# Accumulating transfers in place of VectorE additions in a Strassen matmul chain

## The chip, the cores and the metric

One core of a Trainium2 chip runs the kernel. The metric is the time of one execution on the device, in microseconds (us). Each run of a kernel gives one time; a median of runs is compared with a median. One execution is also recorded by the hardware profiler; its span goes from the first to the last instruction.

## The reference, cut to what matters

```python
# attention: 4 batches, 12 heads, 448 positions, 64 per head
scores = cap * tanh(q @ k.T / sqrt(64) / cap); attn = softmax(scores); x = attn @ v
# mixer 1: over tokens, then over channels (768 -> 1536 -> 768)
u  = x + (relu(x.T @ w_tok1) @ w_tok2).T
x  = u + relu(u @ w_ch1) @ w_ch2
# mixer 2: real part of a two-dimensional FFT, normalization, channels (768 -> 3072 -> 768)
u  = x + real(fft(fft(x, axis=1), axis=2))
un = (u - mean(u)) / sqrt(var(u) + 1e-6)
out = u + relu(un @ w_ch1) @ w_ch2
```

All of it is fp32.

## The kernel before

An fp32 product is made of three matmuls at reduced precision: each factor is split into a high part and a low part (`wh`, `wl` for weights; `u`, `r`, `y` tiles for activations), and `mm3` (L300 to L303) adds high x high, high x low and low x high in PSUM. The split takes one copy on ScalarE (L329) and one subtraction (L332) on VectorE or, where the planner prefers it, on GpSimd.

The stages follow each other: attention with the token mixer (to about 300 us), the first channel mixer, the FFT as matmuls with tables, and the second channel mixer. The result accumulates in SBUF in `z`: 12 tiles `z[bp][kc]` of 128 channels x 2 x 448 positions, `bp` being a pair of batches, `kc` one of six groups of channels. When a PSUM tile `mm` is complete, `gather` (L1555) adds it to `z`, on VectorE: the instruction z<-mm,z.

The second channel mixer does its first pair of batches as ordinary products and, for the second pair, uses Strassen's scheme: seven products in place of eight, per group of hidden channels `g`. `up_steps(g)` makes the seven hidden operands out of sums and differences, `down_steps(o, g)` the seven products with the second weight. While this second half runs, the tiles `z[0][...]`, whose own result has been stored, serve as accumulators `a` for products that belong into more than one place:

- products 1 and 5 collect in `a = z[0][kc]`, kc = 0 to 2 (`a[:, 0, :]` and `a[:, 1, :]`); 
- products 6 and 7 collect in `a = z[0][NJ + kc]`, with NJ = 3.

The accumulators are then folded into `z[1]`. At the end of the group before the last, `fold_in` (L1597) adds the two halves of `a` to each other and the whole of `a` to `z[1][kc]` and to `z[1][NJ + kc]`; `fold_out` (L1604) does likewise for products 6 and 7. In the last group the accumulators start from zero again, and `last15` (L1612) and `last67` (L1622) copy the first PSUM half into `a` (ScalarE), add the second (VectorE), and fold. `last23` (L1633) gathers products 2 and 3 and stores; product 4 goes by `one` (L1586). Each store waits for all additions to its tile.

No engine's program is written out by hand. All operations are first listed with what they read and write, and a planner (`Plan.run`, L187) then picks the next one again and again: it has a cost for each operation on each engine, a lag until the result of a transfer can be used, and starts whatever can begin first. Ties and near ties go by a rank, the place in the list shifted by the tables `SHIFT` (by stage) and `FINE` (by 64 operations of a kind). It counts a cost for TensorE's change between kinds of matmul (`LEAVE`, `ENTER`, L224) and keeps GpSimd apart from VectorE's instructions on SBUF. Each engine then works through its list in order, waiting for semaphores. GpSimd's list holds the maxima over partitions of attention, a part of the subtractions, and eight loads of FFT tables (L841, L857), the only transfers that it issues; all others are issued by SyncE (SP).

Of the kernel before, what the change touches and what calls it, by code (L numbers as in the profile page):

```python
# [56 lines left out]
class Op:  # L57
# [8 lines left out]
    None: -2, "acc0": -4454, "acc1": 433, "all": 12, "all<": -585, "all>": 551, "av": 161, "av<": -4361,  # L66
# [3 lines left out]
    "den>": -1057, "dev0": -4528, "dev1": -728, "exp": 272, "exp<": -611, "exp>": -1228, "fold00": 27,  # L70
    "fold01": -173, "fold02": -771, "fold10": -37, "fold11": 219, "fold12": -777, "gather": -43, "hid": -327,
    "late": 605, "load": -427, "load<": 151, "load>": -1918, "max": 70, "max<": -6696, "max>": -3403,
    "mean0": -1187, "mean1": -6750, "mix1": 211, "mix2": 266, "mix1>0": -3128, "mix1>1": -150, "mix2>1": 113,
    "mixh": -1004, "mixh>0": -68, "mixh>1": 41, "norm": -902, "norm<": 288, "norm>": -2108, "piece": -88,
    "recip": -63, "recip<": -608, "recip>": -179, "row0": -5, "row1": -1713, "scores": -39, "scores<": -1930,
    "scores>": -120, "spec00": -4598, "spec01": -978, "spec10": 399, "spec11": 251, "su0": 326, "su1": -368,
    "sub": -237, "sub<": -271, "sub>": -7902, "tanh": 187, "tanh<": -2194, "tanh>": 145, "tmm00": 130,
    "tmm01": -1093, "tmm10": 311, "tmm11": -1096, "tok1": 276, "tok2": -2798, "tokens00": -28, "tokens01": -5846,
    "tokens02": 2, "tokens10": 224, "tokens11": -318, "tokens12": -4780, "turn": -5524, "turn<": -1352,
    "turn>": -3039, "wx": -65, "xt": -5606, "xt<": -991, "xt>": -3434,  # L80
}
FINE = {
# [42 lines left out]
class Plan:  # L125
# [10 lines left out]
    LEAVE = {"rows": 0.11, "cols": 0.08}  # L136
    ENTER = 0.09
# [125 lines left out]
def kernel(  # L263
# [67 lines left out]
    def tt(engs, out, in0, in1, op, reads, writes):  # L331
        pl.op(engs, lambda e: eng[e].tensor_tensor(out=out(), in0=in0(), in1=in1(), op=op), reads, writes)  # L332
# [411 lines left out]
    def phase_ce():  # L744
# [851 lines left out]

        def fold_in(kc):  # L1597
            a, zl, zh = z[0][kc], z[1][kc], z[1][NJ + kc]
            ka = zk(0, kc)
            tt(v(S), lambda: a[:, 1, :], lambda: a[:, 1, :], lambda: a[:, 0, :], ALU.add, ka[:1], ka[1:])  # L1600
            for x, k in ((zl, kc), (zh, NJ + kc)):
                tt(v(W2), lambda x=x: x, lambda x=x: x, lambda: a, ALU.add, ka, zk(1, k))

        def fold_out(kc):  # L1604
            a, zl, zh = z[0][NJ + kc], z[1][kc], z[1][NJ + kc]
            ka = zk(0, NJ + kc)
            tt(v(S), lambda: zl[:, 1, :], lambda: zl[:, 1, :], lambda: a[:, 0, :], ALU.add, ka[:1], zk(1, kc)[1:])
            tt(v(S), lambda: a[:, 1, :], lambda: a[:, 1, :], lambda: a[:, 0, :], ALU.add, ka[:1], ka[1:])
            tt(v(W2), lambda: zh, lambda: zh, lambda: a[:, 1:2, :].to_broadcast([128, 2, S]), ALU.add, ka[1:],
               zk(1, NJ + kc))  # L1610

        def last15(kc, ps):  # L1612
# [6 lines left out]
            for x, k in ((zl, kc), (zh, NJ + kc)):  # L1619
                tt(v(W2), lambda x=x: x, lambda x=x: x, lambda: a, ALU.add, ka, zk(1, k))  # L1620
# [257 lines left out]
```

## Time and profile before

| | us |
|---|---|
| median of 3 runs | 1386.49 (1384.38 to 1386.78) |
| the profiled execution | 1383.64 |
| its span | 1381.9 |
| TensorE (PE) busy | 1359.3 |
| VectorE (DVE) busy | 973.6 |
| ScalarE (ACT) busy | 713.3 |
| GpSimd (POOL) busy | 300.7 |

PE is the engine of matmuls, PEld its weight loads, which run beside it. A matmul's own duration overlaps with the next one's, so the pace is read from start to start. In a row of the timeline stand start, duration, engine, line, operation, out<-in and, in brackets, idle time of the engine before it and what ended it. Where several like instructions stand in one row, x2 tells their number and the duration is that of all. The granted clock of TensorE is 1.00 at its upper level, 2.4 GHz, and 0.50 at the lower, 1.2 GHz.

### The profile page before, as it was taken

The page shows a single profiled execution, that of the slowest core. Times are in us where ns is not written, and L with a number is a line of the kernel's source. Part 1 is how long each engine was busy: PE and PEld are TensorE (multiplying, and loading weights), DVE is VectorE, ACT ScalarE, POOL GpSimd, SP SyncE. Part 2 cuts the span into 40 slices and gives each one's busy share as a digit, 9 for nine tenths or more (in the row PEclk, how much of TensorE's full clock was granted, in tenths as well). Part 3 has the DMA queues.
Part 4 walks back from the last instruction along what each step waited for, and adds up shares of the span by engine and source line. Part 5 has one row for each costly group of instructions (what it writes and reads, how often), then busy time and mean ns, then how long its engine had stood idle before and what let it go on. Part 6 is the DMA issues. An engine that isn't in the chain of part 4 may idle for free.

```text
span 1381.9 us, 18670 instructions
## 1 busy us (share of the span) xinstructions
PE 1359.3 (98%) x7470; PEld 1133.6 (82%) x7470; DVE 973.6 (70%) x1006; ACT 713.3 (52%) x836; POOL 300.7 (22%) x159
## 2 busy tenths in 40 slices
PE   8899999999999999999999999999999999999997
PEld 3345454589999999899989989999999999999987
DVE  7898787745564555658888687677676646756697
ACT  7888887766566444123223335544554553543432
POOL 3342342300000001000002242425123313212311
PEclk9999999999999999999999999999999999999999
DMA  4221321025666465512241177988778433344452
GB/s 125 89 74 54 105 63 54 21 92 161 227 236 220 161 229 187 166 67 92 69 160 58 42 256 269 334 276 309 249 257 299 133 117 102 105 129 144 126 181 94
DMA packets 67352, 211.89 MB, mean 153 GB/s; under 512 B 7552, under 2 KB 8960, under 8 KB 67266
## 3 DMA queue, kind: packets, MB, share of 16 engines
q1 hardware_dynamic: 66112, 208.08, 45.1%
q0 software_dynamic: 1152, 2.62, 0.7%
q8 instruction: 59, 0.97, 0.3%
q14 instruction: 27, 0.22, 0.0%
q10 hardware_dynamic: 2, 0.00, 0.0%
HBM read 145.30 MB, written 65.37 MB: 152 GB/s over the span
## 4 chain that ended last, share of the span: by engine, by line
PE 95%; ACT 2%; DVE 1%; DMA 1%; issue 0%; DVEq 0%; ACTq 0%
PE mm L301 25%; PE mm L303 25%; PE mm L302 25%; PE av L588 6%; PE sc L520 5%; PE av L604 3%; PE mx L715 2%; DMA wl<-kept 1%; ACT t L525 1%; PE av L615 1%; PE mx L711 1%; PE mx L301 1%; PE mx L303 1%; PE mx L302 1%; ACT t L545 1%; DVE z L332 1%
## 5 line engine op out<-in xcount | busy, mean ns | idle before, releaser
L303 PE MATMUL mm<-u,wl 128*128 128x448 f32 x786 | 287.2, 365 | 1.6 <-DMA wl<-kept 1.6
L301 PE MATMUL mm<-u,wh 128*128 128x448 f32 x786 | 287.6, 366 | 0.9 <-issue 0.7
L302 PE MATMUL mm<-u,wh 128*128 128x448 f32 x780 | 285.5, 366 | 0.0
L332 DVE TENSOR_TENSOR z<-mm,z 128x896 f32<-128x896 f32 (+1 forms) x211 | 214.8, 1028 | 79.3 <-PE mm L303 76.6
L301 PE MATMUL mm<-r,wh 128*128 128x448 f32 x696 | 254.7, 366 | 0.3 <-ACT wh L329 0.3
L303 PE MATMUL mm<-r,wl 128*128 128x448 f32 x696 | 254.5, 366 | 0.3 <-DVE wl L332 0.3
L302 PE MATMUL mm<-r,wh 128*128 128x448 f32 x654 | 239.1, 366 | 0.0
L303 PEld LDWEIGHTS mm<-u,wl 128*128 128x128 f32 x786 | 147.6, 188 | 14.3 <-DMA wl<-kept 2.0
L301 PEld LDWEIGHTS mm<-u,wh 128*128 128x128 f32 x786 | 147.6, 188 | 14.0 <-issue 1.4
L302 PEld LDWEIGHTS mm<-u,wh 128*128 128x128 f32 x780 | 146.5, 188 | 11.8
L301 PEld LDWEIGHTS mm<-r,wh 128*128 128x128 f32 x696 | 130.8, 188 | 11.9 <-ACT wh L329 0.6
L303 PEld LDWEIGHTS mm<-r,wl 128*128 128x128 f32 x696 | 130.7, 188 | 11.4 <-DVE wl L332 0.7
L537 POOL PARTITION_ALL_REDUCE mb<-m x48 | 95.9, 2049 | 169.6 <-DVE m L332 149.1
L302 PEld LDWEIGHTS mm<-r,wh 128*128 128x128 f32 x654 | 122.9, 188 | 10.4 <-DVE r L332 0.4
L329 ACT ACTIVATE r<-mm 128x896 fp32r<-128x896 f32 (+5 forms) x85 | 70.0, 828 | 109.0 <-PE mm L303 56.7
L329 ACT ACTIVATE cva<-raw 128x768 bf16<-128x768 int8 (+2 forms) x76 | 67.4, 887 | 96.1 <-DMA raw<-in_m_dram 49.2
L332 DVE TENSOR_TENSOR t<-t,mb 112x1792 f32<-112x1792 f32 x48 | 105.5, 2228 | 8.6 <-POOL mb L537 8.6
L332 POOL TENSOR_TENSOR wl<-wl,wh 128x768 fp32r<-128x768 f32 x18 | 36.1, 2008 | 344.1 <-ACT wh L329 344.1
L525 ACT ACTIVATE t<-sc,scl 112x896 f32<-112x896 f32 x96 | 93.1, 1010 | 17.0 <-PE av L604 8.1
L329 ACT ACTIVATE wh<-wl 128x768 fp32r<-128x768 f32 x57 | 48.2, 845 | 93.9 <-DMA wl<-kept 92.1
L520 PE MATMUL sc<-qr 64*112 64x448 f32 x384 | 89.5, 576 | 6.2 <-ACT t L525 5.2
L545 ACT ACTIVATE t<-t,cap_sb 112x1792 f32<-112x1792 f32 x48 | 85.6, 1791 | 10.8 <-DVE t L332 10.6
(203 smaller groups left out, 2158.3 us busy)
## 6 DMA issues: line engine op xcount, KB each, us to landing
raw<-in_m_dram SPq DMA_DIRECT2D x48, 767.6 KB, 5.2
wl<-kept SPq DMA_DIRECT2D x85, 384.0 KB, 3.6
kept<-u SPq DMA_DIRECT2D x60, 384.0 KB, 5.0
raw<-in_c_dram SPq DMA_DIRECT2D x24, 767.6 KB, 5.4
kept<-y SPq DMA_DIRECT2D x32, 384.0 KB, 5.3
raw<-kept SPq DMA_DIRECT2D x31, 384.0 KB, 3.1
wh<-kept SPq DMA_DIRECT2D x28, 384.0 KB, 3.3
qr<-in_qk_dram SPq DMA_DIRECT2D x23, 448.0 KB, 3.3
```

What stands on the lines that cost most here:

```text
L301: T.matmul(out=dst, lhsT=wh, rhs=xh, start=first, stop=False, skip_group_check=more)
L302: T.matmul(out=dst, lhsT=wh, rhs=xl, start=False, stop=False, skip_group_check=more)
L303: T.matmul(out=dst, lhsT=wl, rhs=xh, start=False, stop=last, skip_group_check=more)
L329: pl.op(a(n), lambda e: A.activation(out=out(), in_=src(), func=func, **kw), reads, writes)
L332: pl.op(engs, lambda e: eng[e].tensor_tensor(out=out(), in0=in0(), in1=in1(), op=op), reads, writes)
L520: T.matmul(out=ps()[:CP, k, :S], lhsT=qr()[d, S + c * CP:S + (c + 1) * CP], rhs=qr()[d, :S], start=True, stop=True)
L525: pl.op(a(W2, 0.06), lambda e, c=c, ps=ps: A.activation(out=tl()[:, c], in_=ps()[:CP, :, :S], func=AF.Tanh, scale=scl[:CP, 0:1]), [ps, tl] ...
L537: pl.op({"P": 1.9}, lambda e, k=k: P.partition_all_reduce(mb()[:, k], mx()[:, k], CP, bass_isa.ReduceOp.max), [mx, mb], [kb], hold=0.75)
L545: pl.op(a(2 * W2, 0.1), lambda e, k=k: A.activation(out=tl()[:, :, k], in_=tl()[:, :, k], func=AF.Exp, scale=cap_sb[:CP, 0:1]), [tl], [ke])
L588: T.matmul(out=ps()[d, :S], lhsT=vv()[:, c, d], rhs=tl()[:, c, hd], start=(c == 0), stop=(c == NCH - 1))
L604: T.matmul(out=ps()[32 * k:32 * k + 32, :S], lhsT=ones[:CP, 0:32].bitcast(F32), rhs=tl()[:, c, hd], start=(c == 0), stop=(c == NCH - 1))
L715: T.matmul(out=ps()[:, :S], lhsT=channels_of(rt()[:, tb, c], kc % NJ), rhs=wt[:, tb, :], start=False, stop=last, skip_group_check=True)
```

## The change

The additions of a whole accumulator, or of one half of it, to a tile of `z[1]` leave VectorE. In their place GpSimd issues a transfer from SBUF to SBUF which adds to its destination. The planner gets a cost of 0.6 us for GpSimd and a lag of 5.0 us. The addition inside `a` stays on VectorE. `SHIFT` and `FINE` (101 and 304 numbers) are replaced throughout, and the costs of a change between kinds of matmul are altered, so all engines' lists are in a new order.

```diff
 SHIFT = {
-    None: -2, "acc0": -4454, "acc1": 433, "all": 12, "all<": -585, "all>": 551, "av": 161, "av<": -4361,
+    None: -2, "acc0": -4783, "acc1": 438, "all": 11, "all<": -387, "all>": 21, "av": 151, "av<": -4659, "av>": 181,
...
 FINE = {
-    "A_0": -211, "A_1": -967, "A_2": -275, "A_3": 2, "A_4": 26, "A_5": -68, "A_6": -37, "A_7": -23, "A_8": 43,
+    "A_0": -75, "A_1": -959, "A_2": -237, "A_3": 17, "A_4": -35, "A_5": -87, "A_6": 35, "A_8": 82, "A_9": -43,
...
-    LEAVE = {"rows": 0.11, "cols": 0.08}
-    ENTER = 0.09
+    LEAVE = {}
+    ENTER = 0.095
...
+        def plus(o, i, reads, writes):
+            pl.op({"P": 0.6}, lambda e: P.dma_start(out=o(), in_=i(), accum_op=ALU.add), reads, writes, lag=5.0)
+
         def fold_in(kc):
...
             for x, k in ((zl, kc), (zh, NJ + kc)):
-                tt(v(W2), lambda x=x: x, lambda x=x: x, lambda: a, ALU.add, ka, zk(1, k))
+                plus(lambda x=x: x, lambda: a, ka, zk(1, k))
 
         def fold_out(kc):
...
-            tt(v(S), lambda: zl[:, 1, :], lambda: zl[:, 1, :], lambda: a[:, 0, :], ALU.add, ka[:1], zk(1, kc)[1:])
+            plus(lambda: zl[:, 1, :], lambda: a[:, 0, :], ka[:1], zk(1, kc)[1:])
             tt(v(S), lambda: a[:, 1, :], lambda: a[:, 1, :], lambda: a[:, 0, :], ALU.add, ka[:1], ka[1:])
-            tt(v(W2), lambda: zh, lambda: zh, lambda: a[:, 1:2, :].to_broadcast([128, 2, S]), ALU.add, ka[1:],
-               zk(1, NJ + kc))
+            plus(lambda: zh, lambda: a[:, 1:2, :].to_broadcast([128, 2, S]), ka[1:], zk(1, NJ + kc))
```

`last15` changes as `fold_in` does, `last67` as `fold_out`. `S` is 448, `W2` 896 columns. Each of the four functions is called for three kc.

## Rows read from the trace of the kernel before

**Rows 1.** The page: busy us of each engine, share of the span, instructions.
```profile
PE 1359.3 (98%) x7470; PEld 1133.6 (82%) x7470; DVE 973.6 (70%) x1006; ACT 713.3 (52%) x836; POOL 300.7 (22%) x159
```

**Rows 2.** Busy time by stretch: stretch, length, busy us (instructions) per engine, clock, DMA.
```profile
0.00:50.00 50.00, 43.26 (x248) 17.40 (x250) 40.77 (x35) 39.11 (x40) 20.93 (x15) 0.97 0.35 106
300.00:1300.00 1000.00, 995.96 (x5044) 917.98 (x5043) 663.28 (x703) 447.11 (x539) 181.94 (x96) 1.00 0.53 179
1300.00:1344.00 44.00, 44.00 (x218) 40.67 (x217) 38.99 (x41) 15.66 (x18) 13.18 (x6) 1.00 0.50 160
1344.00:1352.00 8.00, 5.31 (x19) 4.42 (x18) 8.00 (x9) 3.89 (x6) 0.00 (x0) 0.79 0.30 109
...
1374.50:1382.00 7.50, 0.04 (x1) 0.00 (x0) 3.75 (x6) 0.00 (x0) 0.00 (x0) 0.78 0.61 234
```

**Rows 3.** Waits of TensorE over the span: us in total, times, longest.
```profile
PE mm L302 <- DVE r L332: 2.7, 1, 2.7
PE mm L303 <- DMA wl<-kept: 1.6, 1, 1.6
```

**Rows 4.** Timeline of TensorE, about 1344 to 1352 us.
```profile
1344.26 0.37 PE L301 MATMUL mm<-y,raw 128*128 128x448 f32 x1
1347.32 0.47 PE L302 MATMUL mm<-r,raw 128*128 128x448 f32 x1 [2.69 <-DVE r L332]
...
1351.05 0.53 PE L301 MATMUL mm<-r,raw 128*128 128x448 f32 x1
1351.42 0.37 PE L302 MATMUL mm<-r,raw 128*128 128x448 f32 x1
```

**Rows 5.** Timeline of VectorE, about 1336 to 1347 us.
```profile
1335.92 1.16 DVE L332 TENSOR_TENSOR z<-mm,z 128x448 f32<-128x448 f32 x2 [1.29 <-PE mm L303]
...
1337.99 2.74 DVE L332 TENSOR_TENSOR u<-u,r 128x896 fp32r<-128x896 f32 x1
...
1344.19 1.08 DVE L332 TENSOR_TENSOR z<-z 128x896 f32<-128x896 f32 x1
...
1346.19 1.08 DVE L332 TENSOR_TENSOR r<-r,y 128x896 fp32r<-128x896 f32 x1
```

**Rows 6.** Timeline of VectorE, 1357 us to the end.
```profile
1357.15 0.62 DVE L332 TENSOR_TENSOR z<-mm,z 128x448 f32<-128x448 f32 x1
...
1363.54 1.31 DVE L332 TENSOR_TENSOR z<-mm,z 128x448 f32<-128x448 f32 x2
...
1374.57 1.16 DVE L332 TENSOR_TENSOR z<-mm,z 128x448 f32<-128x448 f32 x2 [1.11 <-PE mm L303]
1375.65 1.61 DVE L332 TENSOR_TENSOR z<-z 128x448 f32<-128x448 f32 x2
1377.18 1.15 DVE L332 TENSOR_TENSOR z<-mm,z 128x448 f32<-128x448 f32 x2
```

**Rows 7.** Timeline of SyncE's issues: two stores, and the last one.
```profile
1375.76 0.81 SPq L1165 DMA_DIRECT2D out_dram<-z  x2
...
1378.35 0.33 SPq L1165 DMA_DIRECT2D out_dram<-z  x1
```

**Rows 8.** VectorE's instructions from 1300 us on, by shape: busy us, mean ns.
```profile
L332 DVE TENSOR_TENSOR z<-z 128x896 f32<-128x896 f32 x18 | 20.8, 1173 | 0.0
...
L332 DVE TENSOR_TENSOR z<-z 128x448 f32<-128x448 f32 x12 | 7.1, 614 | 0.0
```

**Rows 9.** GpSimd: its issues (ns min/median/max), landings (the 399 KB pair; KB, us), a split.
```profile
L857 POOL DMA_DIRECT2D raw<-in_fft_dram x4: 527/543/859, 545.8 to 552.9; - x4
...
DMA to landing us min/median/max: 8.4/9.6/10.9
...
raw<-in_fft_dram POOLq DMA_DIRECT2D x2, 196.0 KB, 3.8
cva<-in_fft_dram POOLq DMA_DIRECT2D x1, 392.0 KB, 4.3
...
1337.62 2.16 POOL L332 TENSOR_TENSOR wl<-wl,wh 128x768 fp32r<-128x768 f32 x1 [2.01 <-ACT wh L329]
```

More of the change, by code (lines that the diff above doesn't have):

```diff
@@ L65 @@
 SHIFT = {
-    None: -2, "acc0": -4454, "acc1": 433, "all": 12, "all<": -585, "all>": 551, "av": 161, "av<": -4361,
[3 rows of a table removed]
[L70 to L80, printed above, removed]
+    None: -2, "acc0": -4783, "acc1": 438, "all": 11, "all<": -387, "all>": 21, "av": 151, "av<": -4659, "av>": 181,
[5 rows of a table added]
+    "load": -2010, "load<": -2536, "load>": -1514, "max": 50, "max<": -5564, "max>": -2576, "mean0": -989,
+    "mean1": -7352, "mix1": 196, "mix2": 290, "mix1>0": -5565, "mix1>1": -991, "mix2>1": -84, "mixh": -1927,
+    "mixh>0": 43, "mixh>1": -1319, "norm": -1593, "norm<": 25, "norm>": -1417, "piece": -87, "recip": 141,
+    "recip<": -2207, "recip>": -1444, "row0": 22, "row1": -1836, "scores": -24, "scores<": -2867, "scores>": -1150,
+    "spec00": -2957, "spec01": -1319, "spec10": 132, "spec11": 522, "su0": 241, "su1": -2092, "sub": -105,
+    "sub<": 230, "sub>": -8213, "tanh": 141, "tanh<": -2205, "tanh>": -27, "tmm00": 44, "tmm01": -2343, "tmm10": 68,
+    "tmm11": -1128, "tok1": 283, "tok2": -4463, "tokens00": -42, "tokens01": -4792, "tokens02": 311,
+    "tokens10": 119, "tokens11": -346, "tokens12": -6875, "turn": -5807, "turn<": 132, "turn>": -1751, "wx": -65,
+    "xt": -4867, "xt<": -2081, "xt>": -3451,
 }
 FINE = {
[39 rows of a table removed]
[39 rows of a table added]
 }
@@ L1619, in last15 @@
             for x, k in ((zl, kc), (zh, NJ + kc)):
-                tt(v(W2), lambda x=x: x, lambda x=x: x, lambda: a, ALU.add, ka, zk(1, k))
+                plus(lambda x=x: x, lambda: a, ka, zk(1, k))
         def last67(kc, ps):
@@ L1628, in last67 @@
             pl.key = None
-            tt(v(S), lambda: zl[:, 1, :], lambda: zl[:, 1, :], lambda: a[:, 0, :], ALU.add, ka[:1], zk(1, kc)[1:])
-            tt(v(W2), lambda: zh, lambda: zh, lambda: a[:, 1:2, :].to_broadcast([128, 2, S]), ALU.add, ka[1:],
-               zk(1, NJ + kc))
+            plus(lambda: zl[:, 1, :], lambda: a[:, 0, :], ka[:1], zk(1, kc)[1:])
+            plus(lambda: zh, lambda: a[:, 1:2, :].to_broadcast([128, 2, S]), ka[1:], zk(1, NJ + kc))
         def last23(kc, ps):
```

84 rows, old and new, of tables (FINE, SHIFT) are left out of this document.

## Prediction

> **What bounds the kernel now.** I read the page's busy shares first, then the busy time of each engine by stretch, then TensorE's waits, and last the instructions around the two places where TensorE stands still. The page has TensorE busy 98% of the span and VectorE 70% [rows 1]. By stretches, TensorE is busy 995.96 of the 1000 us from 300 to 1300 us, at full clock: nothing that VectorE gives up there can be worth more than the remaining 4 us [rows 2]. What is left lies at three places: 6.7 us of the first 50 us, 2.7 us of the eight from 1344 to 1352, and all of the last 7.5 us [rows 2]. Of TensorE's waits, the longest single one is 2.7 us, for VectorE's r, once [rows 3].
>
> That wait is the hand-over from the last but one Strassen group to the last. L301 starts at 1344.26, its successor L302 only at 1347.32 [rows 4]. VectorE is busy without a gap from 1335.92 until the r that L302 needs is written: the subtraction that starts at 1346.19 [rows 5]. In this chain stand three additions z<-z of 896 columns (like the one at 1344.19; the others start at 1336.99 and 1340.65), which nothing in it needs; they are fold_in's and fold_out's. After the wait the granted clock of the stretch is 0.79 [rows 2]: the engine idled 2.7 us, then worked for a time at the lower level (1.2 GHz), and matmuls started 0.37 us apart instead of 0.20 until the row at 1351.42 [rows 4]. From 1344.26 to 1351.42 there are 13 starts; at the pace of the stretch just before (44.0 us for 218 matmuls, 0.20 each [rows 2]) they need 2.6 us and took 7.16. So this place costs 4.5 us, of which 2.85 is the wait (3.06 from start to start, less one pace) and 1.7 the clock.
>
> The end: VectorE takes the last PSUM result at 1374.57, when TensorE is done; it does two additions from mm, two z<-z (448 and 896 columns) and two more additions from mm, until 1378.33 [rows 6]. Stores go out at 1375.76 and, the last, at 1378.35 [rows 7]. 3.5 us later the span ends.
>
> **The change, part by part.** Removed from VectorE: per kc fold_in loses two additions of 896 columns, last15 two, fold_out and last67 one of 896 and one of 448. With three kc that is 18 of 896 and 6 of 448. From 1300 us on the trace has exactly 18 z<-z of 896 columns, mean 1173 ns, and 12 of 448, mean 614 [rows 8]; the other six of 448 are the additions inside a, which stay. Freed: 18 x 1.173 + 6 x 0.614 = 24.8 us of VectorE, about half before 1348 us, half after.
>
> At the hand-over the three additions of 896 are 1.0 us apart from their successors, so the chain behind 1335.92 becomes 3.0 us shorter [rows 5]. The r of 1346.19 would then be ready at 1344.27 instead of 1347.27, and L302 is due at 1344.46: the wait goes, and with it the reason for the low clock. Gain 4.5 us. Nothing spare is left (0.2 us); what is late next is the same chain, and a rest of a few tenths may stay. Shorter waits show no low clock: the stretch from 300 to 1300 has the clock at 1.00, with a wait of 1.6 us for a weight in it [rows 2, 3].
>
> At the end the two z<-z between the gathers go (1.6 us by the rows), and so does the backlog behind which the last two gathers stood. The last stores are then those that follow TensorE's last matmul: as now, 1374.57 plus two additions of 0.55 us, stores at 1375.76 and, behind it on SP, 1376.14 (SP's issues are 0.33 long with 0.05 after each) [rows 6, 7]. From 1378.35 to 1376.14 is 2.2 us.
>
> Added: 24 transfers on GpSimd's queue. One issue takes 0.54 to 0.58 us by the table loads, the only transfers GpSimd issues now [rows 9]; 24 are 13 us, spread over some 60 of the last 82 us; in the first 44 of these GpSimd is busy 13.18 us [rows 2]; they are hidden as long as none waits in front of work that TensorE needs. On SyncE's queue nothing is added; its stores wait for gathers, as now.
>
> How long an accumulating transfer takes to land, the trace doesn't show. From below: the smallest table load, 196 KB, 3.8 us; from above: the pair of table loads that took 9.6 in the median and 10.9 at worst, doubled, since the destination is read as well: 21.8 [rows 9]. The nearest row is a 392 KB load to 128 partitions at 4.3; I scale it to 448 KB (4.9) and add two fifths for the second read: 7 us. Does that fit? In z the additions are chained: last15's transfer into a tile must land before last67's into the same tile is issued, then the gather, then the store. The last operand of last15 is ready at about 1357.8 (the row at 1357.15), its two transfers are out by 1358.9; the last of last67's operands is ready at 1364.85 (the row at 1363.54, two additions) [rows 6]. With landing time L the gather is free at 1358.9 + 2L + 0.55 or at 1364.85 + 1.1 + L, whichever is later: with L = 7 both are about 1373, before TensorE's last result. Up to L = 8 it is hidden; each us beyond costs two.
>
> The Trainium skill (DMA: Bandwidth & Descriptors, Anatomy of one DMA) gives such a transfer about 2.0 us plus its bytes at 436 GB/s, an estimate of 3.1 us for these 448 KB. The table loads are slower than that in this trace, and the sum does not use it; by it the end would be hidden with room to spare.
>
> The order: SHIFT, FINE and the switch costs are new, so the whole program is laid out anew, the attention stage too, where no transfer is added. There the first 50 us hold 6.7 us of idle TensorE [rows 2]; I take 0, with an estimate of 3 us lost or won (half of those 6.7 us).
>
> **Sum.** 4.5 + 2.2 = 6.7 us. The profiled execution took 1383.64 us (span 1381.9 and 1.7 around it); after: 1376.9. The median of the runs shown is 1386.49, 2.85 above the profiled one; against it I forecast 1386.49 - 6.7 = 1379.8. A measurement of this kernel tells about 0.2% (2.8 us) from no change.
>
> **Rivals.** (a) Transfers land late, L from 8 to 11 us: last67's transfers stand on GpSimd until last15's have landed, the gathers of the last tiles and their stores wait. At L = 10.9 the gather is free at 1381.3, the last store at 1381.9, 3.5 us after today's; less the 4.5 of the hand-over that is 1 us faster: 1385.5. For it: the two loads at 9.6 [rows 9]. Against it: these have 113 partitions, the one of 128 took half.
>
> (b) GpSimd's issues hold up VectorE. A subtraction u<-u,r took 2.74 us beside a GpSimd subtraction from 1337.62, and one of the issues took 859 ns beside VectorE's work [rows 5, 9]. If each issue held VectorE for its 0.55 us, three of them in the chain would give back 1.65 of the 3.0 us: a wait of 1.5 to 1.6 us stays, the clock is kept (as after the one wait of 1.6 us [rows 3]), and the gain is 2.9 at the hand-over and 2.2 at the end: 1381.4. The Trainium skill speaks against (b) (SBUF — State Buffer, Who interferes with whom): a VectorE instruction with two inputs in SBUF contends with a GpSimd instruction that reads SBUF; writing a transfer's descriptors needs, as the page infers, the write side alone. The 2.74 us agree with its first half; the second no row shows. It also means that removing z<-z, all with two inputs in SBUF, takes away work that GpSimd can hold up.
>
> (c) Slower: a transfer that waits in GpSimd's in-order queue, for an operand or for an earlier landing, stands in front of a weight split (2.16 us of GpSimd [rows 9]) that TensorE is due to use. TensorE then idles by what is left of L = 7 after the split's lead, and the clock falls: with a lead of 2 us, 5 + 1.7 us. Two such, in place of the one wait removed, are 13.4 - 6.7 = 6.7 us slower: 1393.2; one gives 1386.5, no change. It decides from a lead under L. For it: GpSimd has splits in just the stretches in which the transfers are issued. Against: the planner leaves 5 us (lag) between an issue and its use, and in its order GpSimd's queue holds other work only if that fits its costs; so only the part of L beyond 5 surprises it.
>
> (d) The change does what it says, and the new order also wins 3 us of the first 50: 1376.8. Or it loses 3 there: 1382.8.
>
> **How the numbers follow.** The forecast 0.48, (a) 0.17, (b) 0.08, (c) 0.17, (d) 0.10. Faster by over 0.2%: forecast, (b), (d) wholly or nearly, and a little of (a): 0.63. Within 0.2%: most of (a), (c) with one such wait: 0.20. Slower: (c) with two or more, and (a) with L beyond 12: 0.17. The likeliest case alone lies between 1377 and 1382 (a rest of the wait, a gather more at the end). The range that holds 8 in 10 is 1375 to 1390: (d) below; above, (a) whole and (c) up to half of its price. What lies beyond is L toward its upper bound of 21.8.
>
> **What would show it.** Right: no VectorE r that TensorE waits over 1 us for near 1340; clock 1.00 in that stretch; VectorE's busy time some 25 us lower; after the last matmul only two additions on VectorE; last store under 2 us behind the last matmul; issues of 0.55 us on GpSimd, landing in 5 to 8. Wrong: stores at the end that wait for a transfer; TensorE waits on wl or raw from GpSimd; a TensorE stretch between 0 and 1300 us that differs by more than 3 us.

## The result and the profile after

The changed kernel takes 1397.51 us (1395.82 to 1399.24, 4 runs), the kernel before, beside it on the same chip, 1386.58 (1384.38 to 1386.78). The ratio is 1.0083 [1.0068, 1.0099]: some 11 us slower. I had forecast 1379.8 and a range up to 1390, so even the sign is wrong. The profiled execution took 1397.01 us, its span is 1394.8, 12.9 longer than before.

The page of after (busy us, share, instructions; then GpSimd's DMA queue: packets, MB, share of 16 engines):

```profile
PE 1361.3 (98%) x7470; PEld 1134.0 (81%) x7470; DVE 963.1 (69%) x994; ACT 712.8 (51%) x836; POOL 287.7 (21%) x171
...
q0 software_dynamic: 5376, 12.26, 4.5%
```

VectorE gave up only 10.5 us over the span [rows 1], not the 24.8 that the additions took: from 300 to 1300 us the new order gives it 9.3 us more and GpSimd 13.5 less (672.56 and 168.43 below, 663.28 and 181.94 in [rows 2]). GpSimd's queue q0 is the new item: 4.5% of the span is 63 us of all 16 DMA engines. On the page of before this queue, with the table loads alone, has 2.62 MB and 0.7%, 9.7 us. So 24 transfers of 9.64 MB take 53 us of all 16 engines, and they do it within the last 80 us.

Busy time by stretch, after (columns as in [rows 2]):

```profile
0.00:50.00 50.00, 43.95 (x254) 16.14 (x254) 40.67 (x35) 41.97 (x43) 22.04 (x16) 1.00 0.38 111
300.00:1300.00 1000.00, 995.42 (x5042) 918.83 (x5041) 672.56 (x709) 446.40 (x539) 168.43 (x90) 1.00 0.54 179
1310.00:1345.00 35.00, 33.34 (x165) 30.52 (x163) 15.24 (x19) 8.14 (x10) 12.49 (x13) 1.00 0.95 252
1345.00:1357.00 12.00, 5.51 (x20) 5.02 (x21) 10.43 (x12) 5.05 (x8) 3.39 (x3) 0.72 0.83 164
1357.00:1390.00 33.00, 24.11 (x107) 21.29 (x105) 12.62 (x17) 5.49 (x8) 11.53 (x12) 0.84 0.98 204
```

Up to 1300 us nothing that matters has moved. Behind it the last column but one is what to look at: the DMA engines are busy 95%, 83% and 98% of the three stretches, against 50% from 1300 to 1344 before [rows 2]. TensorE stands still for a part of the last two, at a lower clock. VectorE is not what is short: 15.24 of 35 us.

TensorE, after, timeline (start, duration):

```profile
1342.98 0.36 PE L301 MATMUL mm<-r,raw 128*128 128x448 f32 x1
1351.49 0.74 PE L302 MATMUL mm<-r,raw 128*128 128x448 f32 x1 [8.14 <-DVE r L332]
...
1375.93 0.37 PE L303 MATMUL mm<-r,raw 128*128 128x448 f32 x1
1384.16 0.71 PE L301 MATMUL mm<-r,wh 128*128 128x448 f32 x1 [7.86 <-DVE z L332]
...
1388.40 0.57 PE L303 MATMUL mm<-r,raw 128*128 128x448 f32 x1
```

These five rows account for the span. The hand-over comes 1.28 us earlier than before (1342.98, not 1344.26), then takes 8.51 from start to start, not 3.06 [rows 4]: +5.45. A second wait near the end, of 8.23 from start to start where 0.20 is the pace: +8.03. From 1384.16 to the last matmul 11 paces take 4.24 us, not 2.2, the clock being at its lower level: +2.0. From the last matmul to the end of the span 6.4 us, 7.7 before: -1.3. The sum is 12.9.

**The hand-over.** TensorE waits for VectorE's r, as before. What held r? All waits of after from 1300 us on (engine, what <- what it waited for: us in total, times, longest):

```profile
ACT wh L329 <- DMA wl<-kept: 22.7, 4, 13.2
DVE z L332 <- DMA z<-z: 16.9, 3, 11.1
POOL z L1598 <- DMA z<-z: 15.1, 6, 5.8
...
DVE u L332 <- POOL raw L332: 9.0, 1, 9.0
```

VectorE itself sat idle for 9.0 us, once. Followed back on ScalarE's and VectorE's timelines of after:

```profile
1332.23 0.95 ACT L329 ACTIVATE r<-y 128x896 fp32r<-128x896 f32 x1
1342.04 0.84 ACT L329 ACTIVATE raw<-raw 128x768 fp32r<-128x768 f32 x1 [8.86 <-DMA raw<-kept]
1342.79 0.94 ACT L329 ACTIVATE u<-u 128x896 f32<-128x896 f32 x1
1343.76 0.95 ACT L329 ACTIVATE r<-u 128x896 fp32r<-128x896 f32 x1
```

```profile
1344.81 1.09 DVE L332 TENSOR_TENSOR u<-u,r 128x896 fp32r<-128x896 f32 x1 [9.02 <-POOL raw L332]
...
1350.35 1.09 DVE L332 TENSOR_TENSOR r<-y,r 128x896 fp32r<-128x896 f32 x1
```

ScalarE's list is in order, and at its head stands the copy of a weight that has not come. Behind it stand the two copies which VectorE's u<-u,r needs. (The profile puts VectorE's wait down to GpSimd's split of that weight, which ended at 1344.78; ScalarE's r<-u ended at 1344.71, and u<-u,r reads that r. Either way the late weight is behind it: GpSimd's split also stands behind ScalarE's copy of `raw`.) At 1350.35 comes the r for which TensorE has been waiting. The fetch was not issued late: SyncE issued it at 1328.53, and its counterpart before at 1329.80. Why it came late, the DMA view of after from 1310 to 1345 us tells (queues; then out<-in, queue, count, KB each, median us to landing, that is from the issue until the data has arrived):

```profile
q0 software_dynamic: 1296, 3.44, 51.8%
q1 hardware_dynamic: 1964, 5.36, 42.8%
...
z<-z POOLq DMA_DIRECT2D x7, 448.0 KB, 9.7
wl<-kept SPq DMA_DIRECT2D x8, 384.0 KB, 6.0
...
raw<-kept SPq DMA_DIRECT2D x3, 384.0 KB, 12.9
```

The same stretch before:

```profile
q1 hardware_dynamic: 2160, 5.90, 52.0%
...
wl<-kept SPq DMA_DIRECT2D x8, 384.0 KB, 3.4
raw<-kept SPq DMA_DIRECT2D x5, 384.0 KB, 3.6
```

GpSimd's transfers took 18 of the 35 us of the DMA engines; the weight fetches were left 15 of the 18.2 that they had used; a fetch of `raw` takes 12.9 us in the median instead of 3.6. The Trainium skill (DMA: Bandwidth & Descriptors, Issuing engines are not separate DMA queues) says it: transfers of all issuers run on the same 16 engines and interleave. This trace agrees: GpSimd's transfers and SyncE's fetches share one 95%.

**The end.** GpSimd's issues of after from 1300 us on (duration ns min/median/max, first and last start; the landings of all 24):

```profile
L1598 POOL DMA_DIRECT2D z<-z x24: 856/1200/1929, 1314.2 to 1377.1; - x24
...
DMA to landing us min/median/max: 4.9/10.8/15.1
```

The chain that ended last, its end (start, us, what), and VectorE there:

```profile
1362.47 14.09 DMA z<-z
1377.11 11.04 DMA z<-z
1388.71 1.08 DVE z L332
```

```profile
1380.04 0.62 DVE L332 TENSOR_TENSOR z<-mm,z 128x448 f32<-128x448 f32 x1 [11.06 <-DMA z<-z]
1383.39 1.62 DVE L332 TENSOR_TENSOR z<-mm,z 128x448 f32<-128x448 f32 x2 [2.73 <-DMA z<-z]
1388.17 2.69 DVE L332 TENSOR_TENSOR z<-mm,z 128x448 f32<-128x448 f32 x4 [3.16 <-DMA z<-z]
```

Two transfers into one tile, 14.09 and 11.04 us, stand in series before the last gathers. And gathers that wait hold their PSUM tiles: TensorE finds none free from 1376 until the gather of 1383.39 is done, and starts at 1384.16.

What makes these transfers slow is other transfers of their kind. The queues of after from 1357 to 1392 us:

```profile
q0 software_dynamic: 2112, 4.82, 78.6%
q1 hardware_dynamic: 856, 2.69, 19.7%
```

Of the twelve of the last group, the first was issued at 1357.77 and landed in 4.9 us; the others, issued up to 1377.11, land one behind the other up to 1388.14, 2.3 us apart in the mean. That is about the engine time of one transfer (53 us / 24 = 2.2).

### The profile page after: what moved, and what is told of

Same layout as the page of the kernel before. It is cut to its first block, busy times and chain, and to the rows that moved or that the text cites. A ratio compares the mean times of both kernels' runs of the same rounds, so it can differ in the third digit from the quotient of the medians.

```text
span 1394.8 us, 18694 instructions
## 1 busy us (share of the span) xinstructions
PE 1361.3 (98%) x7470; PEld 1134.0 (81%) x7470; DVE 963.1 (69%) x994; ACT 712.8 (51%) x836; POOL 287.7 (21%) x171
## 4 chain that ended last, share of the span: by engine, by line
PE 88%; DMA 5%; DVE 3%; ACT 2%; issue 1%; POOL 0%; DVEq 0%; ACTq 0%; POOLq 0%
PE mm L301 23%; PE mm L303 23%; PE mm L302 23%; PE av L588 4%; PE sc L520 4%; PE mx L715 2%; PE av L604 2%; DMA z<-z 2%; DMA wl<-kept 1%; PE av L615 1%; DMA raw<-in_m_dram 1%; DMA raw<-kept 1%; PE mx L301 1%; ACT t L525 1%; PE mx L711 1%
## 5 line engine op out<-in xcount | busy, mean ns | idle before, releaser
L537 POOL PARTITION_ALL_REDUCE mb<-m x48 | 87.0, 1861 | 176.4 <-DVE m L332 176.4
L332 POOL TENSOR_TENSOR wl<-wl,wh 128x768 fp32r<-128x768 f32 x14 | 27.2, 1948 | 336.2 <-ACT wh L329 336.2
```

The costliest lines, as they stand in the source:

```text
L537: pl.op({"P": 1.9}, lambda e, k=k: P.partition_all_reduce(mb()[:, k], mx()[:, k], CP, bass_isa.ReduceOp.max), [mx, mb], [kb], hold=0.75)
```

## The experiments

My theory behind the result, F in the expectations: the transfers' use of the DMA engines is the cost; it delays the weight fetches at the hand-over and the transfers themselves at the end. Rivals: the new order (O); the planner's wrong lag and cost (L); GpSimd's issue time (Q); additions in `z` that wait for each other's landings (D). Each ratio is to the kernel before, run beside it, with its 95% interval.

**order_alone: the new order, additions on VectorE.**

```diff
         def plus(o, i, reads, writes):
-            pl.op({"P": 0.6}, lambda e: P.dma_start(out=o(), in_=i(), accum_op=ALU.add), reads, writes, lag=5.0)
+            n = 448 if len(writes) == 1 else W2
+            tt(v(n), o, o, i, ALU.add, reads, writes)
```

> The new tables and switch costs stay; the 24 additions go back to VectorE. Theory F (the 16 DMA engines are full: 24 accumulating transfers keep them busy for some 53 us of the last 80, so weight fetches and the transfers themselves land late): both long waits of TensorE go, time within 3 us of the kernel before (1384 to 1390). Rival O (the new order is what costs): the time stays near 1397.

1386.71 us against 1385.09, ratio 1.0014 [1.0004, 1.0025]: the order costs some 2 us of the 11 (0.6 to 3.5 by the interval). TensorE's wait at the hand-over is that of before:

```profile
PE mm L302 <- DVE r L332: 2.7, 1, 2.7
```

**old_order_transfers: the transfers in the order of before** (`SHIFT`, `FINE`, `LEAVE`, `ENTER` as before).

> The old tables and switch costs, with the 24 transfers and their planner costs. Theory F: 8 to 14 us slower than the kernel before (1394 to 1400), with waits of 5 us or more at the hand-over and at the end. Rival O: within 3 us of the kernel before.

1399.84 us, ratio 1.0111 [1.0090, 1.0132], with waits of TensorE of 8.1 and 8.6 us at the same two places. The transfers bring the loss in either order.

**plain_copy: the same 24 transfers, issued alike, without the addition.**

```diff
-            pl.op({"P": 0.6}, lambda e: P.dma_start(out=o(), in_=i(), accum_op=ALU.add), reads, writes, lag=5.0)
+            pl.op({"P": 0.6}, lambda e: P.dma_start(out=o(), in_=i()), reads, writes, lag=5.0)
```

> The changed kernel, all lists in the same order, but the 24 transfers overwrite their destination instead of adding to it (so z is left wrong). GpSimd issues as many, and as much is written, but no destination is read. Theory F: the queue's share of the engines falls from 4.5% to about 3%, landings from 10 us to 5 or 6, the weight fetch before the hand-over lands in under 8 us instead of 13, and the time falls to 1384 to 1390. Rival Q (GpSimd's issues of 0.9 to 1.2 us and its in-order queue cost the time, not the moving of the data): landings stay above 8 us and the time above 1394.

1374.59 us (1373.86 to 1375.09), ratio 0.9926 [0.9911, 0.9941]: 10.5 us faster than before, with VectorE's list and all transfers in their places. That is more than 9 us below the range I had expected; landings, queue share and weight fetch came out as expected. From 1300 us on no wait of TensorE is listed. Its queue on the page, its issues, and its busy time by stretch:

```profile
q0 software_dynamic: 3168, 12.26, 2.6%
```

```profile
L1598 POOL DMA_DIRECT2D z<-z x24: 536/555/753, 1313.0 to 1358.7; - x24
...
DMA to landing us min/median/max: 2.8/5.5/7.4
```

```profile
1310.00:1345.00 35.00, 35.00 (x172) 31.79 (x172) 23.66 (x28) 11.98 (x15) 10.13 (x14) 1.00 0.83 295
...
1345.00:1360.00 15.00, 15.00 (x75) 13.84 (x74) 10.13 (x14) 6.78 (x10) 7.03 (x12) 1.00 0.86 322
```

The same bytes take 2.6% of 1372.4 us less the 9.7 of the tables, 26 us, half of what the accumulating ones took. They land in 5.5 us, and their issues are those of the forecast. A fetch of `raw` takes 6.1 us from 1310 to 1345. So the addition in the transfer, not the transfer's being there, separates 10 us faster from 11 us slower.

**handover_only and end_only: transfers in one half.** In the first, `fold_in` and `fold_out` use transfers and `last15` and `last67` VectorE; the second is the reverse.

> Only fold_in and fold_out use transfers (12); the additions of the last group are back on VectorE. Theory F: TensorE's wait at the hand-over stays at 6 us or more, since the weight fetch before it shares the engines with the transfers, the wait 30 us later goes; 1388 to 1392. If the chain of two landings at the end were the whole cost: 1380 to 1386.

1389.09 us against 1383.90, ratio 1.0041 [1.0028, 1.0054]. TensorE's waits from 1300 us on:

```profile
PE mm L302 <- DVE r L332: 8.3, 1, 8.3
PE mm L302 <- POOL r L332: 1.7, 1, 1.7
```

> Only last15 and last67 use transfers (12); fold_in and fold_out are back on VectorE. Theory F: hand-over as in the kernel before (a wait of 2 to 4 us), and at the end gathers that wait for landings of 10 us and a wait of TensorE of 4 to 8 us; 1390 to 1395. If the hand-over were the whole cost: 1384 to 1388.

1395.26 us, ratio 1.0078 [1.0062, 1.0095], just above what was expected.

```profile
PE mm L301 <- DVE z L332: 7.9, 1, 7.9
PE mm L302 <- DVE r L332: 2.7, 1, 2.7
```

Each half brings its own long wait and not the other's; neither is a gain. The two losses don't add (0.41% and 0.78%, together 0.83%, where the order is in all three); that they overlap was not followed up.

**true_costs: the planner told what the trace shows.**

```diff
-            pl.op({"P": 0.6}, lambda e: P.dma_start(out=o(), in_=i(), accum_op=ALU.add), reads, writes, lag=5.0)
+            pl.op({"P": 0.9}, lambda e: P.dma_start(out=o(), in_=i(), accum_op=ALU.add), reads, writes, lag=12.0)
```

> The changed kernel with a lag of 12.0 us and 0.9 us of GpSimd per transfer in the planner, as measured, in place of 5.0 and 0.6. Theory F: the engines are as full as before, so the planner can hide little of it: 1391 to 1400. Rival L (only the planner's lag was too short): the waits go, 1380 to 1387.

1397.22 us, ratio 1.0094 [1.0079, 1.0109]: as slow as the change. The wait for a PSUM tile is gone, that for r is not, and the last gather only starts at 1390.12:

```profile
PE mm L302 <- DVE r L332: 9.5, 2, 8.8
```

The planner moves the wait; the load stays (the DMA engines are busy 94% from 1310 to 1345 us), since the planner has a lag for a transfer and no share of the DMA engines.

**traffic_only: the kernel before, all additions on VectorE, plus 24 plain transfers of the accumulators** to memory that nothing reads.

```diff
+        def copies(a, ka):
+            for n in range(2):
+                k = home(W2)
+                pl.op({"P": 0.55}, lambda e, k=k: P.dma_start(
+                    out=homes[k], in_=a.rearrange("p a s -> p (a s)").bitcast(I32)), ka, [("home", k)], lag=5.0)
+                pl.extra.append(pl.ops.pop())
```

It is called twice in `fold_in`, by its loop over two tiles, and twice in `fold_out`, for three kc each. `pl.extra` keeps these operations out of the numbering by which `SHIFT` and `FINE` are applied.

> The kernel before, all additions on VectorE; beside fold_in and fold_out GpSimd issues 24 plain transfers of an accumulator (448 KB each) to memory that nobody reads, two for each of the 12 accumulating ones there, so that they take about as much of the DMA engines. No addition waits for a transfer. Theory F (full engines delay the weight fetch before the hand-over): that fetch lands in over 8 us instead of 3, TensorE waits 4 us or more at the hand-over, 1387 to 1394. Rival D (the wait comes from additions in z that wait for each other's landings): the fetch may be late, but the wait stays near 2.7 us and the time within 2 us of the kernel before.

1406.46 us against 1383.35, ratio 1.0164 [1.0143, 1.0186]: more than any theory gave. The place is the theory's. DMA from 1310 to 1345 us, ScalarE behind its weight, and TensorE's longest waits from 1300 us on:

```profile
q0 software_dynamic: 1341, 7.74, 55.1%
...
wl<-kept SPq DMA_DIRECT2D x7, 384.0 KB, 10.7
raw<-kept SPq DMA_DIRECT2D x5, 384.0 KB, 8.4
```

```profile
1348.45 0.84 ACT L330 ACTIVATE raw<-raw 128x768 fp32r<-128x768 f32 x1 [11.20 <-DMA raw<-kept]
```

```profile
PE mm L302 <- ACT wh L330: 7.1, 1, 7.1
PE mm L302 <- DVE z L333: 5.7, 4, 2.5
```

Traffic alone, with the tables of before and no addition moved, makes weights late and TensorE wait at the hand-over, so rival D is not needed for that. Why the loss is so large was not followed up. These transfers go to DRAM and take 55% of the stretch, where plain_copy's take 36%; and VectorE, which is relieved of nothing here, runs late afterwards: its four waits of the second row lie behind 1364 us, where the DMA engines are no longer full (26% from 1360 to 1410).

**plain_halves: plain copies cut in two, 48 issues.**

```diff
-            pl.op({"P": 0.6}, lambda e: P.dma_start(out=o(), in_=i()), reads, writes, lag=5.0)
+            def halves_of(e):
+                x, y = o(), i()
+                c = x.shape[-1] // 2
+                for s in (slice(0, c), slice(c, 2 * c)):
+                    P.dma_start(out=x[..., s], in_=y[..., s])
+
+            pl.op({"P": 0.6}, halves_of, reads, writes, lag=5.0)
```

> The kernel with plain copies, each cut into two of half the columns: as many bytes, twice the issues, 48 (z is left wrong as there). Theory F: the time stays within 3 us of the one with whole plain copies (1373 to 1378). Rival Q (GpSimd's time for an issue, which an accumulating transfer nearly doubles, makes the waits): a large part of the 23 us between plain and accumulating transfers comes back, over 1382.

1376.64 us, ratio 0.9953 [0.9936, 0.9971]; plain_copy had 0.9926. 24 more issues, some 13 us of GpSimd, cost some 4 us by these ratios (8 at the ends of the intervals). The changed kernel's issues are longer than plain_copy's by about as much, 24 x 0.65 = 15 us, so issue time is a minor part of the 22 us between those two: some 4 us, 8 at most.

**three_transfers, three_again, six_transfers: few transfers in the order of before.** In `fold_out` the addition to `zh` becomes a transfer, three in all (cost 0.9, lag 10); the third kernel does so in `last15` too.

```diff
-            tt(v(W2), lambda: zh, lambda: zh, lambda: a[:, 1:2, :].to_broadcast([128, 2, S]), ALU.add, ka[1:],
-               zk(1, NJ + kc))
+            plus(lambda: zh, lambda: a[:, 1:2, :].to_broadcast([128, 2, S]), ka[1:], zk(1, NJ + kc))
```

> The old tables, and of the 24 additions only three as transfers: those of fold_out to the upper half of z, which stand in the chain of VectorE before the hand-over. Theory F: three transfers are some 8 us of the DMA engines, in a stretch of 35 us where half of them is free; the weight fetches land in under 6 us, TensorE's wait at the hand-over falls under 1.5 us, and the kernel is 2 to 5 us faster than the one before (1382 to 1385). If any accumulating transfer there delays the fetch: 1387 to 1392.

> The kernel with three transfers once more, for a narrower interval: 1 to 4 us faster than the kernel before.

> Three more transfers, last15's additions to the upper half of z, in a stretch in which the DMA engines are busy 18%; the additions of last67 to the same tiles stay on VectorE and must wait for a landing of about 9 us. Theory F: VectorE's backlog at the end shrinks by 3 us, the last store goes out 1 to 2 us earlier, 1 to 2 us faster than with three. If the wait for the landing takes its place: the same as with three, or 1 to 3 us slower.

Three, the same kernel twice: ratios 0.9988 [0.9975, 1.0000] and 0.9990 [0.9975, 1.0005], each not told from no change. By them it is 1.7 and 1.4 us faster, where 2 to 5 and then 1 to 4 were expected. Six: 1380.53 us against 1383.35, ratio 0.9982 [0.9972, 0.9993], 2.5 us (0.18%) faster than before, so it beats the kernel before and the changed one; whether it beats three isn't settled. Of three_transfers the waits of TensorE from 1300 us on, and the stretch before the hand-over:

```profile
PE mm L301 <- ACT z L329: 1.3, 1, 1.3
```

```profile
1310.00:1345.00 35.00, 35.00 (x172) 32.02 (x172) 31.04 (x36) 9.80 (x11) 6.54 (x5) 1.00 0.64 181
```

With the DMA engines at 64% the weight fetches come nearly at their old pace (3.9 us for `raw`, 4.4 for `wl`), the VectorE chain is shorter, and the 2.7 us wait is gone, the clock kept.

## Why the prediction was wrong

**What bounds the kernel, and what VectorE's relief is worth: right.** In plain_copy the wait for r goes and the clock stays at 1.00, as the step on the hand-over said. Its last 130 matmuls (from the 130th last start to the last) take 26.7 us, before 30.7: 4.0, forecast 4.5. From the last matmul to the end of the span it has 4.6 us, before 7.7: 3.1, forecast 2.2. The 130th last starts 2.4 us earlier; I gave the order 0 plus or minus 3. These three are the 9.5 us between the spans; the third was not forecast, and what brings it was not followed up.

**The cost of the added transfers: the step that failed.** I let it be hidden whole, and it came to some 22 us, the distance from plain_copy. It had two terms, issues and landing. The issues were taken, from the rows of plain transfers, as 0.54 to 0.58 us; they took 0.86 to 1.93. The landing L was taken as 7 from one table load and "hidden up to 8"; it was 10.8 in the median and 15.1 at worst. My own formula for the last gather, 1358.9 + 2L + 0.55, gives 1384.6 with L = 12.6, the mean of the chain's 14.09 and 11.04; it was 1388.17, since the first of the two went out at 1362.47. My upper bound of L, 21.8, held all this. But L is no constant of one transfer, as the formula has it: the first of the last group landed in 4.9 us, below my 7, and those behind it in up to 14.1, since they wait for one another in the DMA engines.

A third term was missing: what the transfers take from the others. It was put at nothing without a reason, and at the hand-over it turned the forecast gain of 4.5 us into a loss of 5.45 (8.51 us from start to start, not 3.06). I counted the DMA column only for the table loads' times and never set 9.64 MB against the 50% already in use [rows 2]. That load is what made `raw` late at the hand-over and L long at the end. With 26 us of plain transfers the engines still carry both (83% from 1310 to 1345 us, `raw` in 6.1 us); with 53 us they don't.

**Rival (a)** had the mechanism of the end, and the chance for slower named it with L beyond 12, which the chain's 12.6 is. But it priced the stores alone: it missed that a gather which waits keeps its PSUM tile, and TensorE stands for 7.9 us. **Rival (c)** had the sign and the form (an in-order queue blocked ahead of a split), and my chance for slower, 0.17, hung mostly on it; but the queue was ScalarE's and its head waited for a weight, not for an accumulating transfer. GpSimd's own head did wait for landings, 15.1 us in six waits, about half before the hand-over and half at the end. No wait of TensorE for GpSimd is listed in after from 1300 us on. **Rival (b)** falls: u<-u,r at 1344.81 took 1.09 us beside two issues from 1344.72 to 1347.19, and 2.74 before beside a GpSimd subtraction [rows 5]. That is as the Trainium skill infers (SBUF — State Buffer, Who interferes with whom). **Rival (d)**: by order_alone the order loses some 2 us, within the 3 that I allowed; the first 50 us, where (d) looked for them, gain 0.7 in after (TensorE busy 43.95, not 43.26).

Not settled: why the addition doubles the DMA engines' time, and why its issue takes twice as long. A second read of the destination would fit the factor, and no run separates it. Smaller packets alone are not the reason: without the table loads the pages count 4224 packets for the accumulating transfers and 2016 for the plain ones, of the same bytes, but a packet of 3584 bytes took 305 ns in the mean in after and 167 in plain_copy.

## What to carry to other kernels

Work moved to transfers is paid in DMA engine time, in the stretch where it runs: add the new transfers' share to the stretch's own share before anything else, and if the sum nears 100%, ask which fetch comes late and what stands behind it in an in-order list. Several transfers in one burst land one behind the other: count their engine time for the last one, not one landing. Price an accumulating transfer at twice a plain one until a trace shows it. A few such transfers, where the DMA engines have room, can win a little (six: 0.18%) where all of them lose (24: 0.83%).

## What the runs showed of the hardware

An accumulating transfer within SBUF took about 2.2 us of all 16 DMA engines (53 us for 24 of 448 and 224 KB), the plain one 1.1 (26 us). Its issue on GpSimd took 0.86 to 1.93 us against 0.54 to 0.75, and it landed in 10.8 us in the median against 5.5. DMA engines that are nearly full do not by themselves stop TensorE: six_transfers has them busy 90% from 1345 to 1357 us, and TensorE at 10.69 of 12 us and full clock (its one wait there, from 1300 us on, is 1.3 us for ScalarE). What counted in the runs was what came late in such a stretch: a weight fetch at the hand-over, the accumulating transfers themselves at the end.

```profile
1345.00:1357.00 12.00, 10.69 (x53) 9.36 (x52) 7.76 (x10) 7.47 (x11) 5.83 (x5) 1.00 0.90 243
```
